# A first off-diagonal product on 32 rows that reads a transpose itself, and copies that carry half

## The chip, the cores and the metric

The kernel runs on one core of one Trainium2 chip. The metric is device microseconds of one execution: lower is better. Before the change the median of three runs is 678.3 us (677.63 to 680.24).

The engines are TensorE (PE in the profile; its weight loads are PEld), VectorE (DVE), ScalarE (ACT), GpSimd (POOL) and SyncE (SP, which issues the DMAs). Each works through its own instructions in order and waits on semaphores for the others.

## The reference

A recurrence over 768 steps for 4 batches of 8 heads of width 40, and behind it a dense layer with a quick GELU:

```python
for t in range(S):                       # S = 768, state is (B, H, 40, 40)
    y[:, :, t] = einsum('bhd,bhde->bhe', rt, state)
    Sa = einsum('bhde,bhe->bhd', state, at)
    state = state * wt[:, :, None, :] - einsum('bhd,bhe->bhde', Sa, bt)
    state = state + einsum('bhd,bhe->bhde', vt, kt)

x = y.transpose(0, 2, 1, 3).reshape(B * S, H * D)   # 3072 x 320
h = x @ w_in                                        # 320 x 2048
out = (h * (1 / (1 + exp(-1.702 * h)))) @ w_out     # 2048 x 320
```

All of it is in float32.

## The kernel before, in words

The steps are cut into 12 chunks of 64, and the batches into 2 pairs; a chunk of a pair is a *unit*, 24 in all. Within a unit the recurrence becomes matrix products: for each of the 16 pairs of batch and head there is a strictly triangular matrix N, 64x64, from the decayed a and b, and the unit needs T, the inverse of the identity plus or minus N. The state goes from one unit to the next of the same pair of batches. After two units (one chunk of all batches) the dense layer of that chunk runs: ps_up, a GELU on ScalarE (L988), ps_down.

*Cut of TensorE.* A tile of a matmul lies on 64 rows (partitions) and 64 columns of the array: a half of the partitions in, a half of the partitions out. Four such matmuls, one for each quarter, run beside each other; the code's HALF and QUARTERS name them. A float32 matmul has two records in the profile.

*The inverse (function inverse, L662 to L833).* The 64x64 matrix is cut into 32x32 blocks. The two diagonal blocks are inverted by five levels (LEVELS = 5, n = 0 to 4) of an iteration:

- Units 4 to 23 (`level`, L736): a product ps_level of EX(n) and W(n) has 64 columns for each of the 8 slots, of which the first 32 serve to make the next factor and the last 32 are T as far as it has come. L751 copies all 64 columns into W(n + 1), L753 makes E(n + 1) from the first 32 straight out of PSUM, `turned` transposes E into ES in 32x32 blocks (L702, VectorE) and spreads ES into EX (L707 on ScalarE, L709 on POOL or VectorE): column block 0 holds ES on the partitions of the upper block and zeros elsewhere, column block 1 the same for the lower block. The mask is `quads`. The last level, n = 4, multiplies the last 32 columns of W alone.
- Units 0 to 3 (`plain_level`, L758): PT holds 96 columns for each slot, a 64-wide square and 32 columns of T. L784 copies all 96 from PSUM, L723 transposes the square out of PSUM into EX. The last level multiplies the last 32 columns of PT alone.

After the last level `turned` is called once more (L790): ES(5) is the transpose of T's two diagonal blocks, and the spread of it goes into the tile T, a block-diagonal 64x64 matrix for each slot. L797 copies the blocks untransposed into Tc.

*The off-diagonal block* is then two small products. `off_one` (L801, ps_Q) multiplies P21, the lower left block of N with the whole 64 rows, by column block 1 of T, that is by ES(5) on the lower 32 rows and zeros on the upper ones. L816 or L818 mask the result into QT, `off_two` (L822, ps_T) multiplies by Tc, and L830 adds the result into T. `solved` (L899, ps_X) then uses T.

*What sets the order.* The tasks are made by `plan.add` with what they read, write and need room for. A list written out in the file (ORDER, 2700 entries) gives their order, the engine of each and the PSUM bank of each; nothing is planned anew when the kernel is built, so the change leaves order, engines and banks as they are. Waits between engines follow from the tiles that the instructions touch. PT, P21, W, E, ES, EX and T have two buffers each, one for even and one for odd units.

Of the kernel before, what the change touches and what calls it, by code (L numbers as in the profile page):

```python
# [248 lines left out]
def rwkv7_gelu_quick(ctx: ExitStack, tc: tile.TileContext, time_d, v_d, w_d, wc_d, ak_d, b_d, rv_d, w_in, w_out, out):  # L249
# [11 lines left out]
    LEVELS = 5  # L261
# [5 lines left out]
    ROUNDS, WINDOW, SHARE = 4, 5000.0, 1.0  # L267
    RANKS = [14, 16, 20, 24, 35, 37, 39, 41]
    HALF = [slice(0, 64), slice(64, 128)]
    CHANNELS = [slice(h.start, h.start + D) for h in HALF]  # L270
    BITS = (0, 1)
    QUARTERS = [(0, 0), (1, 1), (0, 1), (1, 0)]
# [7 lines left out]
    plan = Plan(dict(logw=3, wc=3, G=1, wch=3, wz=2, time=2, ak=2, b=2, rv=2, FT=3, GT=1, kh=2, bh=2, zr=2, rz=2,  # L280
                     A=1, B=1, RV=2, E0=2, W0=2, P21=2, PT=2, W=2, E=2, ES=2, EX=2, T=2, Tc=1, QT=1, zraw=2, zT=1, M=2, x=1, xT=3, g=4, ob=1), 4)
# [12 lines left out]
    def psum(t, name):  # L294
        if t.pair not in psums:
            psums[t.pair] = banks.tile([128, 2, 512], FP32, tag=f"pair{t.bank}", name=name)
        return psums[t.pair]

    def mm(o, lhsT, rhs, start):
        nc.tensor.matmul(o, lhsT, rhs, start=start, stop=True, skip_group_check=True)  # L300
# [5 lines left out]
    def pe(*sets):  # L306

        return {"PE": sum(n * 2 * max(m[0] / 1.2 + 5 if m else 58.0, cols / 1.2 + 3) for n, cols, *m in sets), "instr": sum(16 * n for n, *_ in sets)}
# [5 lines left out]
    def dve(n):  # L314
        return {"DVE": 170.0 + 1.03 * n}

    def act(n):
        return {"ACT": 210.0 + 0.76 * n}

    def any2(n):  # L320
        return {**act(n), **dve(n)}

    def copy(e):
        return nc.scalar.copy if e == "ACT" else nc.vector.tensor_copy
# [33 lines left out]
    nc.gpsimd.memset(edges, 1.0)  # L358
    for p in HALF:
        q = slice(p.start, p.start + MID)  # L360
# [17 lines left out]
    for t, one in (upper, 1.0), (later, -1.0):  # L378
        nc.gpsimd.memset(t, one)
        for p in HALF:  # L380
            select(t[p, :64], ALU.is_gt, 0, 1, 0.0)
# [24 lines left out]
    P21_t, Tc_t = several("P21", [128, 8 * 32]), several("Tc", [128, 5 * 32])  # L406
# [4 lines left out]
    EX_t, T_t, QT_t = several("EX", [128, 8, 2, 32]), several("T", [128, 8, 2, 32]), several("QT", [128, 8, 32])  # L411
# [83 lines left out]
    def load(i):  # L495
        for name, of, src, n in (("ak", ak_of, ak_d, 1024), ("b", b_of, b_d, 512), ("rv", rv_of, rv_d, 1024),
                                 ("RV", RV_of, v_d, 320), ("time", time_of, time_d, 2 * DM)):
            rows = [slice(p.start, p.start + D) for p in HALF] if name in ("ak", "b", "rv") else [slice(0, 128)]

# [38 lines left out]
    def decay(i):  # L538
# [3 lines left out]
        def by_time(t):  # L542
            ps, lw = psum(t, "ps_cum"), logw_of(i)
            for n in (1, 0):
                for b in BITS:
                    u = b ^ n
                    mm(ps[HALF[u], b, :160], incl[HALF[b]], lw[HALF[b], n * 160:(n + 1) * 160], True)
        plan.add(R, pe((1, 160)), by_time, reads=T("log"), uses=T("logw"), room=T("G"), writes=T("cum"), pair=("cum", i))

        def by_channel(t):  # L550

            ps = psum(t, "ps_cumc")
            for u, f in product(BITS, BITS):
                for b, e in QUARTERS:
                    o, h = (2 * u + f) * 65, head(e, f, b, u) * D
                    mm(ps[HALF[e], b, o:o + 65], logw_t[i % 3][HALF[b], h:h + 64], edges[HALF[b]], o == 0)

# [46 lines left out]
    at = lambda tiles, n: tiles[n % len(tiles)]  # L604
# [8 lines left out]
    def prep(i):  # L613
# [16 lines left out]
        def score_A(t):  # L630

            ps = psum(t, "ps_A")
            for b, f in product(BITS, BITS):
                for e, u in QUARTERS:
                    o, j = (2 * b + f) * 64, slot(b, u, f)
                    mm(ps[HALF[u], e, o:o + 64], khT()[CHANNELS[e], j], ahT()[CHANNELS[e], j], o == 0)
        plan.add(R + 1, pe((4, 64)), score_A, reads=T("khT", "ahT"), uses=T("ak"), room=T("A"), pair=("A", i))
# [4 lines left out]
        def score_RV(t):  # L642

            ps, rv = psum(t, "ps_RV"), rv_of(i)
            for e, b in product(BITS, BITS):
                for f, u in QUARTERS:
                    o, j = (2 * e + b) * 128, 4 * u + 2 * e + b
                    mm(ps[HALF[u], f, o:o + 64], rv[CHANNELS[f], 1, j], rv[CHANNELS[f], 0, j], o == 0)
        plan.add(R + 1, pe((4, 64)), score_RV, reads=T("rv"), room=T("RV"), pair=("RV", i))
# [12 lines left out]
    def inverse(i):  # L662
        R = 10 * i - 5
        T = lambda *names: [(n, i) for n in names]
        ahT = lambda: ak_of(i)[:, 0]
        blocks = lambda ps, n: ps[:, :, :4 * n].rearrange("p r (j t) -> p r j t", t=n)
        tiles_of = lambda t: t.rearrange("p (r j) t -> p r j t", r=2)
        every = lambda t, shape: t.unsqueeze(1).unsqueeze(1).to_broadcast(shape)
        W, E, ES, EX = (lambda n, t=t, k=k: at(t, turn(i, n, k)) for t, k in ((W_t, 5), (E_t, 5), (ES_t, 6), (EX_t, 5)))
        key = lambda name, n, k: (name, turn(i, n, k))  # L670
        within_of = lambda n: within[:, n].bitcast(UINT32)

        PT = at(PT_t, i).rearrange("p (j t) -> p j t", t=96)
# [62 lines left out]
        def level(n):  # L736
            first, last = n == 0, n == LEVELS - 1
            wide, rank = 32 if last else 64, R + 0.5 + 0.5 * n

            def go(t):  # L740
                ps, x, w = psum(t, "ps_level"), EX(n), at(W0_t, i) if first else W(n)
                for k in range(4):
                    for r, q in QUARTERS:
                        mm(ps[HALF[q], r, k * wide:(k + 1) * wide], x[HALF[r], index(n, r, q, k)].rearrange("p n t -> p (n t)"),
                           w[HALF[r], index(n, r, q, k), 64 - wide:], k == 0)
            pair = ("L", turn(i, n, 5))
            plan.add(rank, pe((4, wide)), go, reads=[key("EX", n, 5)] + (T("W0") if first else [key("W", n, 5)]),
                     room=T("T", "Tc") if last else [key("E", n + 1, 5)], pair=pair)
            if last:
                return pair  # L750
            plan.add(rank, any2(512), lambda t: copy(t.engine)(tiles_of(W(n + 1)), blocks(psum(t, ""), 64)),  # L751
                     writes=[key("W", n + 1, 5)], pair=pair)
            plan.add(rank, dve(256), lambda t: nc.vector.tensor_sub(  # L753
                tiles_of(E(n + 1)), every(two32, [128, 2, 4, 32]), blocks(psum(t, ""), 64)[:, :, :, :32]),
                     writes=[key("E", n + 1, 5)], pair=pair)
            turned(rank, lambda t: E(n + 1), dict(reads=[key("E", n + 1, 5)]), n + 1, EX(n + 1), [key("EX", n + 1, 5)])

        def plain_level(n):  # L758
            last = n == LEVELS - 1
            wide, rank = 32 if last else 96, R + 0.5 + 0.5 * n  # L760

            def go(t):
                ps, x = psum(t, "ps_level"), square(n)
                for k in range(4):
                    for r, q in QUARTERS:
                        mm(ps[HALF[q], r, k * wide:(k + 1) * wide], x[HALF[r], index(n, r, q, k)],
                           PT[HALF[r], index(n, r, q, k), 96 - wide:], k == 0)
                for r, q in QUARTERS:
                    first, hi, lo = index(n, r, q, 0), index(n, r, q, 2) - index(n, r, q, 0), index(n, r, q, 1) - index(n, r, q, 0)
                    of_k = PT[HALF[r], :, 64:].rearrange("p (a b c) t -> p a b c t", a=2, b=2)  # L770
                    bits = {4: 0, 2: 1, 1: 2}
                    fixed = 7 - hi - lo
                    picks = [slice(None)] * 5
                    picks[1 + bits[fixed]] = int(bool(first & fixed))
                    got = of_k[tuple(picks)]
                    if hi < lo:
                        got = got.rearrange("p a b t -> p b a t")
                    mm(ps[HALF[q], r, :4 * wide].rearrange("p (a b t) -> p a b t", a=2, b=2)[:, :, :, wide - 32:], ident[HALF[r]], got, False)
            pair = ("L", turn(i, n, 5))
            plan.add(rank, pe((4, wide), (1, 128)), go, reads=[key("EX", n, 5), ("PV", turn(i, n, 5))], uses=T("PT"),  # L780
                     room=T("T", "Tc") if last else [], pair=pair)
            if last:
                return pair
            plan.add(rank, any2(768), lambda t: copy(t.engine)(tiles_of(PT), blocks(psum(t, ""), 96)),  # L784
                     writes=[("PV", turn(i, n + 1, 5))], pair=pair)
            turned_square(lambda t: blocks(psum(t, ""), 96)[:, :, :, :64], dict(pair=pair), n + 1)

        for n in range(LEVELS):
            pair = plain_level(n) if i < PLAIN else level(n)
# [11 lines left out]
        def off_one(t):  # L801

            ps = psum(t, "ps_Q")
            for e in BITS:
                for b, u in QUARTERS:
                    j = 4 * u + 2 * e
                    mm(ps[HALF[u], b, e * 64:e * 64 + 64].rearrange("p (f t) -> p f t", f=2), at(P21_t, i)[HALF[b], 128 * e + 64 * u:128 * e + 64 * u + 64],
                       at(T_t, i)[HALF[b], j:j + 2, 1], e == 0)
        plan.add(R + 3.5, pe((2, 64)), off_one, reads=T("P21", "T0"), room=T("QT"), pair=("Q", i))

        def upper_rows(t):
            src = psum(t, "")[:, :, :128].rearrange("p b (e f t) -> p b e f t", e=2, f=2)
# [9 lines left out]
        def off_two(t):  # L822

            ps, QT = psum(t, "ps_T21"), at(QT_t, i).rearrange("p (b e f) t -> p b e (f t)", b=2, e=2)
            for e in BITS:
                for u, b in QUARTERS:
# [6 lines left out]
                 reads=T("T0"), writes=T("T"), pair=("T21", i))  # L833
# [296 lines left out]
```

## Time and profile before

| | |
|---|---|
| median of 3 runs | 678.3 us |
| the profiled execution | 678.87 us, span 677.2 us |
| TensorE busy | 650.6 us, 96% |
| TensorE's weight loads | 561.3 us, 83% |
| VectorE, ScalarE, POOL busy | 447.1, 330.6, 175.0 us |
| mean granted TensorE clock | 0.989 |
| ps_up and ps_down on the chain that ended last | 31% each |

A row of a group reads: line, engine, operation, tiles written and read, shapes, count, then busy microseconds and mean nanoseconds of one, then the idle time of that engine before them and what ended it. A row of the timeline begins with its start and its length in microseconds. A row of a stretch gives the busy time of each engine in it, the granted clock of TensorE as a share of full speed, the DMA engines' share and GB/s. Matmuls are recorded on L300, the helper `mm`, so they are told apart by their tiles. Their ends are modelled.

### The profile page before, as it was taken

How to read it: one execution, taken by the hardware profiler on the slowest of the kernel's cores; microseconds unless marked ns; L12 is line 12 of the kernel's file. 1: busy time of each engine (PE TensorE's matmuls, PEld its weight loads, DVE VectorE, ACT ScalarE, POOL GpSimd, SP SyncE). 2: the span in 40 equal slices, each digit the busy share in tenths (PEclk: the TensorE clock that was granted, in tenths of full speed). 3: DMA queues.
4: the chain of work that ended last, by engine and by line, in shares of the span. 5: the costliest groups of instructions: out<-in, count | busy, mean ns of one | idle time of the engine just before them, and what ended most of it. 6: DMA issues, size and time to landing. Idle time of an engine off the chain costs nothing.

```text
span 677.2 us, 42176 instructions
## 1 busy us (share of the span) xinstructions
PE 650.6 (96%) x19488; PEld 561.3 (83%) x19488; DVE 447.1 (66%) x906; ACT 330.6 (49%) x688; POOL 175.0 (26%) x204
## 2 busy tenths in 40 slices
PE   5668999999999999999999999999999999999997
PEld 5567887987987888898998898787988799899895
DVE  5686887777768668667776687868556766675001
ACT  4675955634664655554545435454454354252110
POOL 6442444224123023124123211321412321300000
PEclk9887999999999999999999999999999999999999
DMA  7883736315324224332304413513412412100100
GB/s 234 295 252 126 235 111 183 103 45 157 111 64 132 84 62 129 106 107 77 113 24 133 139 34 108 155 33 107 145 34 72 126 46 63 53 14 29 45 12 20
DMA packets 35311, 69.72 MB, mean 103 GB/s; under 512 B 5440, under 2 KB 14656, under 8 KB 35136
## 3 DMA queue, kind: packets, MB, share of 16 engines
q1 hardware_dynamic: 35136, 67.03, 32.6%
q8 instruction: 153, 2.51, 1.5%
q14 instruction: 22, 0.18, 0.1%
HBM read 59.15 MB, written 7.86 MB: 99 GB/s over the span
## 4 chain that ended last, share of the span: by engine, by line
PE 94%; ACT 2%; DVE 2%; issue 1%; DMA 1%; DVEq 0%; ACTq 0%; SPq 0%
PE ps_up L300 31%; PE ps_down L300 31%; PE ps_level L300 9%; PE ps_y L300 5%; PE ps_B L300 5%; PE ps_X L300 2%; PE ps_A L300 2%; PE ps_rz L300 2%; PE ps_N L300 2%; PE ps_RV L300 2%; PE ps_zT L300 1%; ACT PT L784 1%; PE ps_cum L300 1%; PE ps_Q L300 1%; PE ps_T L300 1%
## 5 line engine op out<-in xcount | busy, mean ns | idle before, releaser
L300 PE MATMUL ps_up<-xT_all,w_sb 64*64 64x256 f32 x3840 | 250.1, 377 | 0.4 <-PE ps_rz L300 0.2
L300 PE MATMUL ps_down<-w_sb,g 64*64 64x320 f32 x3072 | 239.5, 430 | 0.3 <-ACT zr L869 0.2
L300 PEld LDWEIGHTS ps_up<-xT_all,w_sb 64*64 64x64 f32 x3840 | 169.6, 133 | 15.3 <-issue 0.8
L300 PEld LDWEIGHTS ps_down<-w_sb,g 64*64 64x64 f32 x3072 | 133.3, 133 | 39.8 <-issue 1.3
L988 ACT ACTIVATE g<-ps_up 128x1024 f32<-128x1024 f32 x48 | 49.2, 1024 | 45.0 <-PE ps_up L300 44.6
L709 POOL TENSOR_TENSOR EX<-ES,quads 128x512 f32<-128x512 f32 x29 | 38.3, 1323 | 113.3 <-DVE ES L702 75.8
L751 ACT COPY W<-ps_level 128x512 f32<-128x512 f32 x56 | 32.7, 585 | 69.7 <-PE ps_level L300 68.0
L300 PEld LDWEIGHTS ps_level<-W,EX 64*64 64x64 f32 x2560 | 58.7, 134 | 5.8 <-DVE T L830 0.2
L300 PE MATMUL ps_level<-W,EX 64*64 64x64 f32 (+1 forms) x2560 | 55.9, 217 | 0.0
L753 DVE TENSOR_TENSOR E<-two,ps_level 128x256 f32<-128x256 f32 x80 | 33.2, 416 | 34.0 <-ACT W L751 30.3
L707 ACT ACTIVATE EX<-ES,quads 128x256 f32<-128x256 f32 x80 | 36.3, 501 | 30.5 <-DVE ES L702 29.9
L619 POOL TENSOR_TENSOR ak<-ak,FT 128x512 f32<-128x512 f32 x16 | 21.4, 1335 | 75.9 <-DMA ak<-in_ak 52.0
L300 PEld LDWEIGHTS ps_level<-PT,EX 64*64 64x64 f32 x1280 | 32.1, 146 | 8.8 <-DVE EX L723 5.7
L300 PE MATMUL ps_level<-PT,EX 64*64 64x64 f32 (+2 forms) x1280 | 34.2, 245 | 5.3 <-DVE EX L723 4.5
L702 DVE STREAM_TRANSPOSE ES<-E 128x256 f32<-128x256 f32 x80 | 35.3, 443 | 4.4
L300 PE MATMUL ps_y<-M,bh 64*64 64x104 f32 (+1 forms) x768 | 35.0, 247 | 2.4 <-issue 2.1
L300 PE MATMUL ps_y<-RV,kh 64*64 64x104 f32 (+1 forms) x768 | 34.8, 247 | 0.0
L891 ACT COPY B<-ps_B 128x416 f32<-128x416 f32 (+1 forms) x34 | 16.5, 491 | 33.8 <-PE ps_B L300 33.6
L300 PEld LDWEIGHTS ps_y<-RV,kh 64*64 64x64 f32 x768 | 28.5, 133 | 2.3 <-DVE M L907 0.5
L300 PEld LDWEIGHTS ps_y<-M,bh 64*64 64x64 f32 x768 | 27.2, 133 | 2.8 <-issue 2.3
L907 DVE TENSOR_TENSOR M<-ps_X,later 128x832 f32<-128x832 f32 (+1 forms) x24 | 23.8, 993 | 8.2 <-PE ps_X L300 8.0
L627 POOL TENSOR_TENSOR kh<-time,G 128x320 f32<-128x320 f32 x18 | 16.1, 892 | 48.5 <-PE ps_y L300 34.6
(131 smaller groups left out, 1092.9 us busy)
## 6 DMA issues: line engine op xcount, KB each, us to landing
ak<-in_ak SPq DMA_DIRECT2D x48, 160.0 KB
rv<-in_rv SPq DMA_DIRECT2D x48, 160.0 KB
time<-in_time SPq DMA_DIRECT2D x24, 320.0 KB
xT_all<-x_dram SPq DMA_DIRECT2D x48, 160.0 KB
wc<-in_wc SPq DMA_DIRECT2D x20, 264.0 KB
logw<-in_w SPq DMA_DIRECT2D x24, 160.0 KB
RV<-in_v SPq DMA_DIRECT2D x24, 160.0 KB
b<-in_b SPq DMA_DIRECT2D x48, 80.0 KB
```

The source lines that it names most:

```text
L300: nc.tensor.matmul(o, lhsT, rhs, start=start, stop=True, skip_group_check=True)
L619: plan.add(R, {"DVE": 690.0, "POOL": 1270.0, "sbuf": True}, lambda t: of(t.engine).tensor_mul(ahT(), ahT(), FT_of(i)), reads=T("ak", "FT") ...
L627: plan.add(R + 4, {"POOL": 870.0, "DVE": 490.0, "sbuf": True}, lambda t, n=n, dst=dst: of(t.engine).tensor_mul(dst(i)[:, :, :D], by_head(t ...
L702: plan.add(rank, dve(256), lambda t: nc.vector.transpose(ES(n), source(t)), writes=[key("ES", n, 6)], **reads)
L707: nc.scalar.activation(dst[:, :, h], ES(n), ACT.Copy, scale=quads[:, h, :1])
L709: of(t.engine).tensor_mul(dst, ES(n).unsqueeze(2).to_broadcast([128, 8, 2, 32]), quads.unsqueeze(1).to_broadcast([128, 8, 2, 32]))
L751: plan.add(rank, any2(512), lambda t: copy(t.engine)(tiles_of(W(n + 1)), blocks(psum(t, ""), 64)), writes=[key("W", n + 1, 5)], pair=pair)
L753: plan.add(rank, dve(256), lambda t: nc.vector.tensor_sub(tiles_of(E(n + 1)), every(two32, [128, 2, 4, 32]), blocks(psum(t, ""), 64)[:, :, ...
L784: plan.add(rank, any2(768), lambda t: copy(t.engine)(tiles_of(PT), blocks(psum(t, ""), 96)), writes=[("PV", turn(i, n + 1, 5))], pair=pair)
L891: plan.add(R, any2(4 * wide), lambda t: copy(t.engine)(dst(), some(psum(t, "")[:, :, :208])), writes=[("Bv", i)] if x and c > 0 else T("B" ...
L907: plan.add(R + 1, dve(8 * wide), lambda t: nc.vector.tensor_tensor(M_of(i)[:, :, :wide].rearrange("p (j b) n -> p b j n", b=2), some(psum( ...
L988: plan.add(-45, {"ACT": 1030.0, "table": "gelu"}, lambda t: nc.scalar.activation(g_of(c * NQ + q).rearrange("p m r n -> p r m n"), psum(t, ...
```

## The change

It has three parts.

1. *Copies behind the fourth level (n = 3).* In units 4 to 23 the copy into W(4) takes the last 32 of the 64 columns, 256 elements a partition and not 512. In units 0 to 3 the copy into PT takes the last 32 of the 96, 256 and not 768. The columns left out have no reader: the last level reads the last 32 alone, and the next factor is made straight from PSUM. 15 of the W copies and 3 of the PT copies are on ScalarE, 5 and 1 on VectorE.
2. *The first off-diagonal product multiplies 32 rows.* Both operands of ps_Q are cut to the lower 32 partitions of each half (LOWER: 32 to 63 and 96 to 127). Its matmuls have 32 rows and 64 columns; with that their place in the array is given as a tile of 32x64 and not 64x64. It still has 8 matmuls a unit of 64 columns.
3. *It reads ES(5) itself* and not the spread of it in T. So the product waits for the transpose (L702), and no longer for the spread (L707 or L709); the next transpose into that ES buffer has to wait for the product.

```diff
+    LOWER = [slice(h.start + 32, h.stop) for h in HALF]
...
-            plan.add(rank, any2(512), lambda t: copy(t.engine)(tiles_of(W(n + 1)), blocks(psum(t, ""), 64)),
+            past = 32 if n == LEVELS - 2 else 0
+            plan.add(rank, any2(512 - 8 * past), lambda t: copy(t.engine)(tiles_of(W(n + 1))[:, :, :, past:], blocks(psum(t, ""), 64)[:, :, :, past:]),
                      writes=[key("W", n + 1, 5)], pair=pair)
...
-            plan.add(rank, any2(768), lambda t: copy(t.engine)(tiles_of(PT), blocks(psum(t, ""), 96)),
+            past = 64 if n == LEVELS - 2 else 0
+            plan.add(rank, any2(768 - 8 * past), lambda t: copy(t.engine)(tiles_of(PT)[:, :, :, past:], blocks(psum(t, ""), 96)[:, :, :, past:]),
                      writes=[("PV", turn(i, n + 1, 5))], pair=pair)
...
             for e in BITS:
                 for b, u in QUARTERS:
                     j = 4 * u + 2 * e
-                    mm(ps[HALF[u], b, e * 64:e * 64 + 64].rearrange("p (f t) -> p f t", f=2), at(P21_t, i)[HALF[b], 128 * e + 64 * u:128 * e + 64 * u + 64],
-                       at(T_t, i)[HALF[b], j:j + 2, 1], e == 0)
-        plan.add(R + 3.5, pe((2, 64)), off_one, reads=T("P21", "T0"), room=T("QT"), pair=("Q", i))
+                    mm(ps[HALF[u], b, e * 64:e * 64 + 64].rearrange("p (f t) -> p f t", f=2), at(P21_t, i)[LOWER[b], 128 * e + 64 * u:128 * e + 64 * u + 64],
+                       ES(LEVELS)[LOWER[b], j:j + 2], e == 0)
+        plan.add(R + 3.5, pe((2, 64)), off_one, reads=T("P21") + [key("ES", LEVELS, 6)], room=T("QT"), pair=("Q", i))
```

## The prediction

> **What bounds the kernel now.** I read four views first: the page, busy time by stretch, the chain that ended last, and the groups of instructions.
>
> ```profile
> span 677.2 us, 42176 instructions
> PE 650.6 (96%) x19488; PEld 561.3 (83%) x19488; DVE 447.1 (66%) x906; ACT 330.6 (49%) x688; POOL 175.0 (26%) x204
> PE   5668999999999999999999999999999999999997
> ```
>
> The second line of digits is TensorE's busy share in fortieths of the span: it is short of nine tenths only in the first four slices, about 68 us, and at the very end. Busy time by stretch says the same in microseconds:
>
> ```profile
> core 0: us, PE busy (x) PEld busy (x) DVE busy (x) ACT busy (x) POOL busy (x), PEclk, DMA share, GB/s
> 0.00:70.00 70.00, 49.15 (x1720) 44.83 (x1724) 46.38 (x76) 41.45 (x107) 32.33 (x61) 0.90 0.71 222
> 70.00:600.00 530.00, 529.17 (x16192) 453.91 (x16186) 380.21 (x777) 273.39 (x558) 142.65 (x144) 1.00 0.33 99
> ```
>
> So there are two kernels in one. From 70 us on TensorE is idle for 0.83 us in 530: whatever VectorE or ScalarE saves there buys nothing, and whatever is added to TensorE's stream is added to the end. Before 70 us TensorE is idle for 20.85 us, units 0 to 3 go through their inverses with little other work beside them, and a shorter chain can count. The chain that ended last agrees:
>
> ```profile
> PE 94%; ACT 2%; DVE 2%; issue 1%; DMA 1%; DVEq 0%; ACTq 0%; SPq 0%
> ```
>
> The profiled execution took 678.87 us against a span of 677.2; the median of the three runs, 678.3, lies 0.6 us below it. The sum is made against 678.9 and then lowered by 0.6.
>
> **The change, part by part.** The groups that it touches, with the one size that stands for the shorter copies (L692 also copies 128x256 out of PSUM):
>
> ```profile
> L751 ACT COPY W<-ps_level 128x512 f32<-128x512 f32 x56 | 32.7, 585 | 69.7 <-PE ps_level L300 68.0 <-DVE E L753 1.5
> L751 DVE COPY W<-ps_level 128x512 f32<-128x512 f32 x24 | 16.3, 684 | 5.9 <-PE ps_level L300 5.2
> L784 ACT COPY PT<-ps_level 128x768 f32<-128x768 f32 x15 | 12.0, 800 | 7.2 <-PE ps_level L300 5.1 <-ACT wch L569 1.0 <-DVE EX L723 0.9
> L692 ACT COPY P<-ps_N 128x256 f32<-128x256 f32 x22 | 8.2, 371 | 23.1 <-PE ps_N L300 21.6 <-DVE PT L716 1.0 <-DVE PT L689 0.3
> L692 DVE COPY P<-ps_N 128x256 f32<-128x256 f32 x2 | 0.8, 412 | 0.0
> L300 PEld LDWEIGHTS ps_Q<-T,P 64*64 64x64 f32 x384 | 11.7, 135 | 3.8 <-ACT T L707 2.2 <-issue 0.2
> L300 PE MATMUL ps_Q<-T,P 64*64 64x64 f32 x384 | 11.3, 220 | 2.0 <-ACT T L707 2.0
> ```
>
> *Shorter copies, units 4 to 23.* One W copy in four shrinks from 512 to 256 elements: 15 on ScalarE by 585 - 371 = 214 ns, 5 on VectorE by 684 - 412 = 272 ns. That is 3.2 and 1.4 us of engine time, all behind a TensorE that does not wait. Worth 0; if the cover were gone, at most those 4.6 us.
>
> *Shorter copies, units 0 to 3.* Four PT copies go from 768 to 256 elements, on ScalarE 800 - 371 = 429 ns each. Unit 0's is on the path:
>
> ```profile
> 30.62 0.80 ACT L784 COPY PT<-ps_level 128x768 f32<-128x768 f32 x1 [0.70 <-PE ps_level L300]
> 31.45 0.72 DVE L723 STREAM_TRANSPOSE EX<-ps_level 128x512 f32<-128x512 f32 x1 [0.89 <-ACT PT L784]
> 32.22 0.67 PE L300 MATMUL ps_level<-PT,EX 64*64 64x32 f32 x32 [0.79 <-DVE EX L723]
> ```
>
> ScalarE, then VectorE, then TensorE, each idle until the one before: 0.43 us comes off here. Unit 1's copy is the same form, but VectorE has another instruction in front of the transpose:
>
> ```profile
> 37.32 0.80 ACT L784 COPY PT<-ps_level 128x768 f32<-128x768 f32 x1
> 37.58 0.48 DVE L830 SCALAR_TENSOR_TENSOR T<-ps_T,quads,T 128x256 f32<-128x256 f32 x1
> 38.15 0.72 DVE L723 STREAM_TRANSPOSE EX<-ps_level 128x512 f32<-128x512 f32 x1
> ```
>
> L830 ends at 38.06, so the transpose gains 0.09, not 0.43. The copies of units 2 and 3 come after 60 us, where TensorE is full. Copies: 0.5 us.
>
> *The wait of the first off-diagonal product.* In all 24 units TensorE stood still for it once, at unit 0 (the tile's own view, then the timeline):
>
> ```profile
>   ACT T L707: 2.0, 1
> ```
>
> ```profile
> 33.65 0.45 DVE L702 STREAM_TRANSPOSE ES<-ps_level 128x256 f32<-128x256 f32 x1
> 34.13 0.91 ACT L707 ACTIVATE T<-ES,quads 128x256 f32<-128x256 f32 x2 [0.52 <-DVE ES L702]
> 34.95 0.39 ACT L404 COPY PT<-one 128x256 f32<-128x256 f32 x1
> 35.09 0.46 PE L300 MATMUL ps_Q<-T,P 64*64 64x64 f32 x16 [1.96 <-ACT T L707]
> 35.24 0.79 ACT L784 COPY PT<-ps_level 128x768 f32<-128x768 f32 x1
> 35.39 0.81 PE L300 MATMUL ps_N<-b,ak 40*64 40x64 f32 x32
> 35.93 0.37 ACT L816 ACTIVATE QT<-ps_Q,quads 128x128 f32<-128x128 f32 x1
> 36.09 0.31 PE L300 MATMUL ps_level<-PT,EX 64*64 64x96 f32 x3
> ```
>
> The product can start when the transpose ends, at 34.10 instead of 35.09. But ScalarE still has the spread, a preset and a PT copy to do in its order, and that copy, which ends at 36.03, is what the product of 36.09 reads; QT stands behind it too. So the 0.99 us is handed back one step later: worth 0, at most 0.99. Early gain together: 0.5 us, bounds 0 and 0.43 + 0.43 + 0.99 = 1.85. The consumer of the spread that is left, L830, now waits for it directly; it was transitively behind it already. The next write into the same ES tile must now wait for the product; it follows unit i + 2's ps_N, which stands behind this product on TensorE through the P21 tile already. No DMA and no POOL work moves.
>
> *32 rows instead of 64.* The product keeps 8 matmuls of 64 columns per unit, so its stream is no shorter: rows do not set the length (a load of 40 rows for ps_rz takes 139 ns, one of 64 rows here 135). But all 9744 matmuls of the kernel before (19488 records, two for each) run on the array cut into 64x64 tiles; the changed program has 192 on 32x64 tiles, in 24 groups of 8, so the cut changes 48 times. No row of before shows a change of cut. This is what a crossing looks like without one, first TensorE, then its weight loads:
>
> ```profile
> 202.84 0.81 PE L300 MATMUL ps_up<-xT_all,w_sb 64*64 64x256 f32 x9
> 203.44 0.44 PE L300 MATMUL ps_Q<-T,P 64*64 64x64 f32 x16
> 203.67 0.64 PE L300 MATMUL ps_up<-xT_all,w_sb 64*64 64x256 f32 x8
> ```
>
> ```profile
> 203.23 0.51 PEld L300 LDWEIGHTS ps_Q<-T,P 64*64 64x64 f32 x16
> 203.62 0.46 PEld L300 LDWEIGHTS ps_up<-xT_all,w_sb 64*64 64x64 f32 x12
> ```
>
> Two overlaps are at stake. The weights of Q are loaded from 203.23 while ps_up's matmuls (to 203.65) still run; and Q's matmuls start at 203.44, 0.21 us before ps_up's end, as the next ps_up does before Q's end (203.67 against 203.88). Low end: 0, nothing is lost. High end: both overlaps of matmuls go, 2 x 0.21 a unit, 24 x 0.42 = 10.1 us. Between them: a change of cut exposes one weight load, 135 ns, and no more: 48 x 0.135 = 6.5 us. I take the middle one, because a load into another cut has to come before its matmul, while the records' ends are modelled, so that the 0.21 us may overstate what is really in flight.
>
> The Trainium skill (TensorEngine Tiling (Array Packing), Tiling Modes, Key Properties) says that changing the tiling mode, and not just the tile, drains the TensorE. It gives no time; taken literally it is the high end, and no run here shows it yet.
>
> Sum: 678.9 - 0.5 + 6.5 = 684.9, less 0.6 for the median: **684.3 us**, slower by 0.9%.
>
> **The rivals.** (a) *Full drain*: a crossing lets every matmul in flight end first, 10.1 - 0.5 = +9.6, 687.9; with the load exposed behind it as well (48 x 0.135) it would reach 694.4. For it: the overlap in the rows above is real work in flight. Against it: the modelled ends. By the Trainium skill's TensorEngine Tiling (Array Packing), Key Properties, it would be this one.
>
> (b) *The crossing is free*: then only the 0.5 us remains, 677.8, no change that can be measured (0.5% is 3.4 us, about what tells runs of this kernel apart). For it: the column cut stays 64, and the 32 rows lie within the 64 of the old tile. This is also the case in which the change does not do what it says: ScalarE and VectorE are relieved where nobody waits for them.
>
> (c) *Faster*: a granted clock that stays up. TensorE runs at half clock after idle stretches:
>
> ```profile
> 57.80:64.70 6.90, 6.40 (x172) 6.36 (x176) 4.16 (x7) 3.65 (x7) 2.00 (x2) 0.51 0.65 203
> ```
>
> If the shorter early chains kept this stretch at full clock, 3.4 us would come off; with 0.5 and a free crossing that is 674.4, faster by 0.6%. It decides only if a crossing costs under 3.9 / 48 = 81 ns. Against it: of the 20.85 us that TensorE idles before 70 us, 0.5 is a small part, and the stretch lies behind units 0 and 1, where that 0.5 arises.
>
> **How the numbers follow.** Forecast (part of the overlap lost, +2.9 to +8) 0.36; full drain 0.27; free crossing 0.25, a part of it with a small price and still within 0.5%; clock 0.06; more than a drain 0.06. Over 0.5% slower: nearly all of the forecast and the drain and the last, less what falls under 3.4 us, 0.64; within 0.5%: 0.28; faster: 0.08. The range 677.0 to 690.0 runs from the free crossing with the upper bound of the early gain nearly reached, to the full drain with a third of the load exposed; the forecast's own is 681 to 686.5.
>
> **What would show it.** Right: from 70 us on, the matmuls of ps_Q start 0.1 to 0.2 us nearer to the end of those before them than the 0.21 us of overlap above, their weight loads no longer begin under ps_up's pass, and the same on leaving; the span from 70 us to the end longer by 24 x 0.27; W copies at 371 and 412 ns behind the fourth level; ps_Q at unit 0 without ScalarE as its releaser, but the ps_level after it only 0.4 us earlier. Wrong: ps_Q groups still 0.23 us from their first matmul to the next group's; a stretch at half clock gained or lost in the first 70 us, which would move the end by more than the copies do; or TensorE idle time that appears behind 70 us on a wait that the change added.

## The result

| | median | runs |
|---|---|---|
| before | 678.95 us | 677.63 to 680.24 |
| after | 685.77 us | 684.97 to 687.17 |

The ratio is 1.0109, with an interval of 1.0086 to 1.0133: 7.4 us slower (5.8 to 9.0); the two medians themselves lie 6.8 us apart. The forecast was 684.3 against a median of then 678.3, 6.0 slower. The profiled execution took 686.01 us; its page:

```profile
span 684.4 us, 42170 instructions
PE 658.5 (96%) x19488; PEld 523.6 (77%) x19488; DVE 444.7 (65%) x906; ACT 326.7 (48%) x688; POOL 174.5 (26%) x204
PE   5787999999999999999999999999999999999997
```

TensorE is busy for 7.9 us more with the same 19488 records, while its weight loads are busy for 37.7 us less: not because there are fewer, or because one is shorter (133 ns at ps_up and ps_down, before and after), but because they lie over one another more, most of all at ps_up (155.7 us busy and not 169.6) and ps_down (112.1 and not 133.3). Why they do so far from ps_Q was not traced. VectorE and ScalarE lost 2.4 and 3.9 us of work, which shows nowhere in the time. By stretch (TensorE, weight loads, VectorE, ScalarE, POOL, clock):

```profile
0.00:70.00 70.00, 49.62 (x1654) 45.01 (x1658) 43.79 (x74) 39.33 (x102) 30.88 (x61) 0.83 0.69 219
70.00:600.00 530.00, 529.49 (x16027) 423.80 (x16024) 376.54 (x770) 268.23 (x555) 142.40 (x143) 1.00 0.33 99
```

Behind 70 us TensorE is as full as before, but gets through 16027 records in the same 530 us and not 16192. What it does there instead shows in the first product of unit 7, first TensorE, then its weight loads:

```profile
206.58 0.82 PE L301 MATMUL ps_up<-xT_all,w_sb 64*64 64x256 f32 x11
207.33 0.46 PE L301 MATMUL ps_Q<-ES,P 32*64 32x64 f32 x16
207.72 0.66 PE L301 MATMUL ps_up<-xT_all,w_sb 64*64 64x256 f32 x8
```

```profile
206.80 0.15 PEld L301 LDWEIGHTS ps_up<-xT_all,w_sb 64*64 64x64 f32 x3
207.33 0.32 PEld L301 LDWEIGHTS ps_Q<-ES,P 32*64 32x64 f32 x16 [0.39 <-issue]
207.72 0.42 PEld L301 LDWEIGHTS ps_up<-xT_all,w_sb 64*64 64x64 f32 x12
```

The loads of ps_Q no longer run under ps_up's pass: they begin at 207.33, together with their matmuls, and ps_up's modelled end is 207.40. On leaving it is the same: 207.72 against an end at 207.79. From ps_Q's start to the next ps_up it was 0.23 us and is 0.39; the overlap with the ps_up ahead was 0.21 us and is 0.07. The wait has no releaser that the profile knows; it appears among the waits of the weight loads as "issue", where before it stood at 0.2 us, once:

```profile
PEld ps_Q L301 <- issue: 5.3, 13, 0.5
```

The start times of the same matmuls in both traces give the price free of everything else: ahead of a ps_Q and behind it, the shift against before grows by 0.328 us (median of units 2 to 23, 0.29 to 0.38, from means over some 30 records on either side; with medians it is 0.32). That is 0.164 us for each change of the array's cut. Between these steps the shift stands still, but for single stalls that one trace has and the other lacks.

The copies and the wait did what they were to do:

```profile
L753 ACT COPY W<-ps_level 128x256 f32<-128x256 f32 x15 | 5.6, 371 | 13.3 <-PE ps_level L301 9.9 <-DVE ES L703 2.3 <-DVE E L755 1.1
L753 DVE COPY W<-ps_level 128x256 f32<-128x256 f32 x5 | 2.1, 418 | 1.1 <-PE ps_level L301 1.0
L301 PE MATMUL ps_Q<-ES,P 32*64 32x64 f32 x384 | 11.3, 233 | 1.0 <-DVE ES L703 1.0
```

371 and 418 ns (371 and 412 were expected), and unit 0's product waits for the transpose on VectorE and no longer for ScalarE.

### The profile page after: what moved, and what is told of

Same layout as the page of the kernel before. It is cut to its first block, busy times and chain, and to the rows that moved or that the text cites. A ratio compares the mean times of both kernels' runs of the same rounds, so it can differ in the third digit from the quotient of the medians.

```text
span 684.4 us, 42170 instructions
## 1 busy us (share of the span) xinstructions
PE 658.5 (96%) x19488; PEld 523.6 (77%) x19488; DVE 444.7 (65%) x906; ACT 326.7 (48%) x688; POOL 174.5 (26%) x204
## 4 chain that ended last, share of the span: by engine, by line
PE 93%; ACT 2%; DVE 2%; issue 1%; DMA 1%; DVEq 0%; ACTq 0%; SPq 0%
PE ps_up L301 31%; PE ps_down L301 30%; PE ps_level L301 10%; PE ps_B L301 5%; PE ps_y L301 5%; PE ps_X L301 2%; PE ps_N L301 2%; PE ps_rz L301 2%; PE ps_RV L301 2%; PE ps_A L301 1%; PE ps_Q L301 1%; PE ps_zT L301 1%; PE ps_cum L301 1%; ACT PT L787 1%; PE ps_T L301 1%
## 5 line engine op out<-in xcount | busy, mean ns | idle before, releaser
L301 PE MATMUL ps_up<-xT_all,w_sb 64*64 64x256 f32 x3840 | 246.6, 378 | 0.2 <-PE ps_rz L301 0.2
L301 PE MATMUL ps_down<-w_sb,g 64*64 64x320 f32 x3072 | 234.2, 430 | 0.3 <-ACT zr L872 0.2
L301 PEld LDWEIGHTS ps_up<-xT_all,w_sb 64*64 64x64 f32 x3840 | 155.7, 133 | 25.7 <-DVE B L897 0.5
L301 PEld LDWEIGHTS ps_down<-w_sb,g 64*64 64x64 f32 x3072 | 112.1, 133 | 56.5 <-issue 0.4
L753 ACT COPY W<-ps_level 128x512 f32<-128x512 f32 (+1 forms) x56 | 29.6, 528 | 69.6 <-PE ps_level L301 65.7
L301 PEld LDWEIGHTS ps_level<-W,EX 64*64 64x64 f32 x2560 | 55.4, 134 | 8.1 <-DVE T L833 0.2
L301 PE MATMUL ps_level<-W,EX 64*64 64x64 f32 (+1 forms) x2560 | 53.5, 217 | 0.0
L894 ACT COPY B<-ps_B 128x416 f32<-128x416 f32 (+1 forms) x34 | 16.5, 494 | 33.7 <-PE ps_B L301 33.4
L690 DVE COPY_PREDICATED PT<-within,ps_N 128x256 f32<-128x256 uint32 x40 | 17.8, 444 | 17.1 <-ACT P L693 11.4
L301 PEld LDWEIGHTS ps_y<-RV,kh 64*64 64x64 f32 x768 | 25.3, 137 | 3.5 <-DVE M L910 0.5
```

The source lines that it names most:

```text
L690: plan.add(R, dve(256), lambda t, n=n: nc.vector.copy_predicated(tiles_of(at(E0_t, i)), every(within_of(n), [128, 2, 4, 32]), blocks(psum( ...
L753: plan.add(rank, any2(512 - 8 * past), lambda t: copy(t.engine)(tiles_of(W(n + 1))[:, :, :, past:], blocks(psum(t, ""), 64)[:, :, :, past: ...
L894: plan.add(R, any2(4 * wide), lambda t: copy(t.engine)(dst(), some(psum(t, "")[:, :, :208])), writes=[("Bv", i)] if x and c > 0 else T("B" ...
```

## The experiments

The theory (A): the whole loss is the 48 changes of cut, some 0.165 us each. The rivals: it comes from the early stretch (B), from reading ES and its waits (C), from matmuls on 32 rows being slow in themselves (D), or only a change in the rows costs (F). E and G, on how the price adds up, come with the runs that test them. Each run is set against runs of the kernel before that were taken beside it:

| run | changes of cut | against before, us | step at ps_Q, us a unit |
|---|---|---|---|
| copies alone | 0 | +0.7 (-0.7 to 2.0) | 0.00 |
| ES read on 64 rows, short copies | 0 | +0.9 (-0.3 to 2.2) | 0.00 |
| the change | 48 | +7.4 (5.8 to 9.0) | 0.33 |
| 32 rows alone | 48 | +7.3 (6.0 to 8.6) | 0.32 |
| half of the matmuls on 32 rows | 48 | +8.8 (7.5 to 10.2) | 0.33 |
| 32 stationary columns | 48 | +11.2 (9.0 to 13.3) | 0.32 |
| both products on 32 rows | 96 | +14.6 (13.4 to 16.0) | 0.33, and 0.32 at ps_T |
| half on 32 rows, two and two | 96 | +16.9 (15.0 to 18.9) | 0.80 |
| half on 32 rows, in turns | 192 | +40.0 (38.1 to 42.0) | 1.77 |

The third column is the ratio's distance from one times the median of before. The step is taken as above, as a median over units 2 to 23. Of the code cuts below, the first is against the changed kernel and the others against the kernel before; they leave out what a product reads by name, and the lengths of the copies.

### The parts, one at a time

*Copies alone*: the product is that of before.

```diff
-                    mm(..., at(P21_t, i)[LOWER[b], ...], ES(LEVELS)[LOWER[b], j:j + 2], e == 0)
+                    mm(..., at(P21_t, i)[HALF[b], ...], at(T_t, i)[HALF[b], j:j + 2, 1], e == 0)
```

> The shorter copies alone; the off-diagonal product is that of the kernel before (64 rows, T). Theory A (the whole loss is the 48 changes of the array's cut, the copies are worth their early half microsecond): 0.3 to 0.6 us below the kernel before, within 0.2%, unit 0's transpose behind the copy 0.4 us earlier, and every ps_Q group 0.23 us from its first matmul to the next group's. Theory B (part of the loss comes from the early stretch, in which the changed kernel came 1.2 us later to the dense layers, because the earlier copies shift the granted clock): 0.5 to 1.5 us above the kernel before, with more than the 13.7 us at half clock that its trace shows.

Measured: no difference; A's gain of 0.3 to 0.6 us is not seen. On its spot the gain is there to the digit. The timeline of unit 0, answering to the three rows at 30.62, 31.45 and 32.22 of before:

```profile
29.82 0.37 ACT L787 COPY PT<-ps_level 128x256 f32<-128x256 f32 x1 [0.69 <-PE ps_level L301]
30.23 0.72 DVE L724 STREAM_TRANSPOSE EX<-ps_level 128x512 f32<-128x512 f32 x1 [0.46 <-ACT PT L787]
31.00 0.67 PE L301 MATMUL ps_level<-PT,EX 64*64 64x32 f32 x32 [0.37 <-DVE EX L724]
```

The copy takes 0.37 and not 0.80 us, VectorE idles 0.46 and not 0.89, TensorE 0.37 and not 0.79. Yet the first matmul of the dense layers starts at 69.5 us, where it started at 69.6. Its row gives the first and the last start; before, this run, the changed kernel:

```profile
L300 PE MATMUL ps_up<-xT_all,w_sb x3840: 372/376/427, 69.6 to 657.9; 64*64 64x256 f32 x192
```

```profile
L301 PE MATMUL ps_up<-xT_all,w_sb x3840: 372/376/427, 69.5 to 658.4; 64*64 64x256 f32 x192
```

```profile
L301 PE MATMUL ps_up<-xT_all,w_sb x3840: 373/376/427, 71.1 to 665.1; 64*64 64x256 f32 x192
```

So nothing of the 0.42 us is left at 70 us; where it goes was not traced. The time alone does not refute B, whose 0.5 to 1.5 us lie inside the interval, but at its upper end of 2.0 us it could not make the loss of 7.4. Nor does the trace look like B: the granted clock of the first 70 us is 0.95, above the 0.90 of before, and the dense layers start no later.

*32 rows alone*: long copies, and the moving operand from T.

```diff
-                    mm(..., at(P21_t, i)[HALF[b], ...], at(T_t, i)[HALF[b], j:j + 2, 1], e == 0)
+                    mm(..., at(P21_t, i)[LOWER[b], ...], at(T_t, i)[LOWER[b], j:j + 2, 1], e == 0)
```

> The 32 rows alone: both operands cut to the lower 32 rows, the moving one still read from T behind its spread, long copies. Theory A (price per change of cut): +6.5 to +8.5 us, each unit 0.33 us later behind its ps_Q than ahead of it, as in the changed kernel. Theory C (the loss comes from reading ES and its waits, not from the rows): within 1 us of the kernel before.

Measured: +7.3 us, the whole loss, with the same step of 0.32, and without the short copies or ES. C falls, and B as the cause of the loss.

*ES read on 64 rows, short copies*: the mask moves from the spread into the copy of P21, and the array keeps its cut.

```diff
-        plan.add(R, any2(256), lambda t: copy(t.engine)(<P21>, <ps_N>), ...)
+        def lower_rows(t):
+            for e in BITS:
+                if t.engine == "ACT":
+                    nc.scalar.activation(dst[:, e], src[:, e], ACT.Copy, scale=quads[:, 1, :1])
+                else:
+                    nc.vector.tensor_scalar(dst[:, e], src[:, e], quads[:, 1, :1], None, ALU.mult)
+        plan.add(R, any2(256), lower_rows, ...)
...
+                    mm(..., at(P21_t, i)[HALF[b], ...], ES(LEVELS)[HALF[b], j:j + 2], e == 0)
```

> Short copies, and the product reads ES itself, but on 64 rows: the copy of P21 is multiplied by the mask of the lower 32 rows, in two instructions, so that the upper rows of ES meet zeros. Same waits as the changed kernel and no change of cut. Theory A: 0 to 1 us below the kernel before, ps_Q groups 0.23 us long, unit 0's ps_Q at the end of the transpose. Theory C (reading ES costs): like the changed kernel, +5 us or more.

Measured: no difference from before (A's 0 to 1 us faster is not met: it is 0.9 us slower, with zero inside the interval), and no step. This run shows what the wait was worth, in the timeline of unit 0:

```profile
33.09 0.40 DVE L709 STREAM_TRANSPOSE ES<-ps_level 128x256 f32<-128x256 f32 x1
33.52 0.91 ACT L714 ACTIVATE T<-ES,quads 128x256 f32<-128x256 f32 x2 [1.05 <-DVE ES L709]
33.55 0.71 PE L301 MATMUL ps_Q<-ES,P 64*64 64x64 f32 x16 [1.54 <-DVE ES L709]
34.63 0.79 ACT L793 COPY PT<-ps_level 128x768 f32<-128x768 f32 x1
35.48 0.76 PE L301 MATMUL ps_level<-PT,EX 64*64 64x96 f32 x12 [0.35 <-ACT PT L793]
```

The product starts beside the spread and not behind it, 0.9 us sooner; the next ps_level still starts when ScalarE's copy ends, at 35.42.

### What a change of cut costs

*Half of the matmuls on 32 rows*: the first four on 32 rows, the last four on 64.

```diff
+                    rows = LOWER if e == 0 else HALF
+                    mm(..., at(P21_t, i)[rows[b], ...], at(T_t, i)[rows[b], j:j + 2, 1], e == 0)
```

> Of the 8 matmuls of each product the first 4 on 32 rows, the last 4 on 64, all from T, long copies: still 48 changes of cut, but half of the matmuls on 32 rows. Theory A (price per change of cut, 0.165 us each): as with all 8 on 32 rows, +6.5 to +8.5 us. Theory D (matmuls on 32 rows are slower in themselves): half of it, +3 to +4 us.

Measured: +8.8 us (a little above A's 6.5 to 8.5), and a step of 0.33 as with all eight. D, which wanted 3 to 4 us, falls: half as many matmuls on 32 rows, the same price.

*Two and two* has `rows = LOWER if b == u else HALF`, *in turns* `rows = LOWER if b == 0 else HALF`.

> Half of the matmuls of each product on 32 rows, in the order 32 32 64 64 32 32 64 64, all from T, long copies: 96 changes of cut and not 48. Theory A (each change costs 0.165 us): +14.5 to +17 us. Theory D (matmuls on 32 rows are slower in themselves, and the number of changes does not matter): as the run with the first half on 32 rows, +9 us.

> The same half on 32 rows, in turns 32 64 32 64 and so on: 192 changes of cut. Theory A: +28 to +33 us, a straight line through the runs with 48 and 96. Theory E (a change costs because the stream in flight has to end, and with one matmul in flight there is less to wait for): below the line, +18 to +27 us. Theory D: +9 us.

Measured: +16.9 and +40.0 us. The first is what A wanted; the second lies well above its line, not below, so E falls, and A as a plain line too. The groups of ps_Q, with half in one piece, two and two, and in turns:

```profile
L301 PE MATMUL ps_Q<-T,P 64*64 64x64 f32 x192 | 8.3, 242 | 0.0
L301 PE MATMUL ps_Q<-T,P 32*64 32x64 f32 x192 | 8.2, 241 | 2.0 <-ACT T L708 2.0
```

```profile
L301 PE MATMUL ps_Q<-T,P 64*64 64x64 f32 x192 | 15.9, 243 | 0.0
L301 PE MATMUL ps_Q<-T,P 32*64 32x64 f32 x192 | 15.9, 241 | 2.5 <-ACT T L708 2.5
```

```profile
L301 PE MATMUL ps_Q<-T,P 64*64 64x64 f32 x192 | 31.9, 247 | 0.0
L301 PE MATMUL ps_Q<-T,P 32*64 32x64 f32 x192 | 31.7, 245 | 3.2 <-ACT T L708 3.2
```

By their records the same 384 are busy for 16.5, 31.8 and 63.6 us, the two forms added (ends are modelled, so they overlap in part). In one piece four matmuls, one in each quarter, run beside each other; two and two leaves half of the quarters empty, in turns three of four. Uncut, the product takes 0.23 us for its four passes of four, 58 ns a pass. Eight passes of two cost four more, 0.23 us a unit, and sixteen of one twelve more, 0.69. Take that off the steps, and (0.80 - 0.23) / 4 = 0.14 and (1.77 - 0.69) / 8 = 0.135 us are left for a change. That reading was tried with *both products on 32 rows*, which has 96 changes and always four matmuls beside each other (ps_Q as in *32 rows alone*; here the second product):

```diff
-                    mm(..., at(Tc_t, i)[HALF[u], 32 * j:32 * j + 64], QT[HALF[u], b, e], e == 0)
+                    mm(..., at(Tc_t, i)[LOWER[u], 32 * j:32 * j + 64], QT[LOWER[u], b, e], e == 0)
```

> Both off-diagonal products on the lower 32 rows, all 8 matmuls of each, from T and QT, long copies: 96 changes of cut, and all four quarters still work beside each other. The second product leaves out the upper 32 rows of its sum. Theory A (each change costs 0.165 us, whatever the product): ps_T 0.33 us a unit later than without, as ps_Q is, +13 to +16 us in all, and less than the 16.9 us of the run with the same 96 changes inside one product. Theory G (that run's price came from the changes alone, not from quarters standing idle): +16 to +18.5 us.

Measured: +14.6 us, and steps of 0.33 at ps_Q and 0.32 at ps_T, 0.65 a unit where two and two took 0.80. A second product pays the same price, and the steps bear the reading out (the two totals alone would not: their intervals touch).

*32 stationary columns*: 64 rows, each matmul split into two of 32 columns, on 64x32 tiles.

```diff
+                    for h in BITS:
+                        mm(ps[HALF[u].start + 32 * h:HALF[u].start + 32 * h + 32, b, ...],
+                           at(P21_t, i)[HALF[b], <columns + 32 * h>:... + 32], at(T_t, i)[HALF[b], j:j + 2, 1], e == 0)
```

> All 64 rows, from T, long copies, but each matmul of the product split into two of 32 stationary columns each, on tiles of 64 rows and 32 columns: 16 matmuls a unit, still 48 changes of cut, now in the columns. Theory A (any change of the cut empties the array): +7 to +11 us, with the first weight load of ps_Q only behind the last matmul before it. Theory F (only a change in the rows does): 0 to +3 us, what the 8 more matmuls cost, and weight loads of ps_Q still under ps_up's pass.

Measured: +11.2 us, just above A's 7 to 11. TensorE and its loads at unit 7:

```profile
207.26 0.81 PE L301 MATMUL ps_up<-xT_all,w_sb 64*64 64x256 f32 x9
208.00 0.46 PE L301 MATMUL ps_Q<-T,P 64*32 64x64 f32 x32
208.38 0.45 PE L301 MATMUL ps_up<-xT_all,w_sb 64*64 64x256 f32 x4
```

```profile
208.00 0.29 PEld L301 LDWEIGHTS ps_Q<-T,P 64*32 64x32 f32 x32 [0.39 <-ACT logw L527]
```

The same picture: loads only at the end of ps_up's pass (208.07), 0.38 us from ps_Q to ps_up, a step of 0.32. So a change in the columns costs what a change in the rows costs, and F falls. One thing stays open: the profiled execution took 687.6 us, which the steps explain, and the four others 691.2 to 692.4. What those did besides has no trace.

### How the price is made up

In the changed kernel the first load behind a crossing can be set against the matmuls ahead of it, whatever their length. Ahead of it are 320 columns (ps_down) and 104 columns (ps_y), each with its TensorE rows and its load:

```profile
314.37 0.99 PE L301 MATMUL ps_down<-w_sb,g 64*64 64x320 f32 x12
```

```profile
315.29 0.21 PEld L301 LDWEIGHTS ps_Q<-ES,P 32*64 32x64 f32 x8 [0.49 <-ACT g L991]
```

```profile
358.25 0.36 PE L301 MATMUL ps_y<-M,bh 64*64 64x104 f32 x8
```

```profile
358.53 0.32 PEld L301 LDWEIGHTS ps_Q<-ES,P 32*64 32x64 f32 x16
```

The modelled ends are 315.36 and 358.61; the loads begin 0.07 and 0.08 us ahead of them, as with 256 columns (0.07) and with ps_Q's own 64 on leaving (0.07). It is so at every crossing of the changed kernel: 71 to 72 ns on entering (unit 0, whose product waits for the transpose, aside) and on leaving, where before it was 262 to 551 ns on entering and 200 to 372 on leaving. With half of the matmuls on 32 rows, where ps_Q ends on 64 rows and leaving changes no cut, it stays at 235 on leaving. So the load waits for the stream ahead to run out, less a fixed 70 ns by which the modelled ends are late or the load may be early. Behind that, the first matmul takes 265 ns in its record where one with its weights already there takes 217, and the next pass starts 107 ns behind it and not 58: some 48 ns of the load's 128 to 133 are not covered. In the single records of the unit at 207 us the last matmul of ps_Q starts at 207.573 and ps_up's first load at 207.718, 145 ns later, where a pass follows a pass at 58: 87 ns for the array to run empty. 87 and 48 make 0.135, as between the small matmuls above. Where the other 0.03 us of the mean of 0.164 lie stays open. The length of the passes ahead does not show as the reason: by the start times, entering costs 0.16 us behind ps_y's 104 columns and 0.16 to 0.21 behind ps_up's 256, leaving 0.16 behind ps_Q's own 64.

## Why the prediction was right, point by point

- *What bounds the kernel.* Right. Behind 70 us a microsecond put into TensorE's stream is a microsecond at the end, nearly: 22 units there at 0.328 make 7.2 us, and between the first and the last start of ps_up lie 594.0 us and not 588.3 (the rows above), 5.7 more. The other 1.5 us are not shown to be handed back. The trace of before has four stalls of 0.4 to 0.55 us, near 291, 320, 469 and 554 us, that the changed kernel's lacks; but the run with the copies alone, which has no change of cut, lacks three of them too (291, 469, 554), so they belong to single executions.
- *Shorter copies, worth 0 in units 4 to 23, 0.5 us early.* The first is right. Of the second the 0.42 us on the spot is right, but nothing of it arrives: the step that failed is that a gain at 32 us reaches 70 us. In the kernels here the first ps_up starts between 68.9 and 71.4 us, whatever was changed; half a microsecond drowns in that.
- *The wait of the product, worth 0.* Right, by the run that reads ES on 64 rows: the 0.9 us is handed back at the next ps_level, behind ScalarE's copy.
- *32 rows, 48 crossings of 0.135 us, 6.5 in all.* Right in place, sign and nearly in size: 0.164, so 24 x 0.328 = 7.9 us, against 7.4 (5.8 to 9.0) in the runs. Wrong in its account. It said that a crossing exposes one weight load and no more. Of the load only some 48 ns show; the larger part is that it does not begin until the stream ahead has run out. The two came to nearly the same number by chance.
- *Rival (a), full drain.* Right in kind: at every crossing looked at, the load waits for the matmuls ahead (71 to 72 ns before their modelled end). The Trainium skill (TensorEngine Tiling (Array Packing), Tiling Modes, Key Properties) says that changing the tiling mode drains the TensorE. These traces agree. Too dear in size: 0.21 us of overlap went by modelled ends, of which 0.07 stays, so 10.1 us should have been 24 x 2 x 0.14 = 6.7. With the 48 ns of load behind each it comes to 9.0, more than the 7.9 of the start times, so this sum, which rests on modelled ends, does not close.
- *Rival (b), the crossing is free.* Refuted by all six runs with crossings.
- *Rival (c), the clock.* It moved, and no run shows that it mattered:

```profile
0.00:70.00 70.00, 44.22 (x1741) 38.72 (x1742) 46.13 (x76) 41.59 (x106) 33.09 (x61) 1.00 0.72 220
```

This is the run with 32 stationary columns: full clock through the whole early stretch (before: 0.90, after: 0.83), and its first ps_up starts at 71.4 us, later than the 69.6 of before. The other traces have no order by the clock either (0.98: 68.9; 0.88: 69.2; 0.83: 71.1).

The expected sights came as described: ps_Q's loads no longer under ps_up, the copies at 371 and 418 ns, ps_level of unit 0 at the end of the copy. Only "0.4 us earlier" did not come: that ps_level started at 36.55 and not 36.09, in an execution whose granted clock was 0.50 from 27.5 to 44.5 us, where before had 0.99.

## What to carry to other kernels

A matmul on fewer rows is not a cheaper matmul, and in a stream with one cut of the array it is a dearer one: two changes of cut cost as much here, 0.33 us, as the whole product takes otherwise and half of it again. Zeros that fill a tile up to the cut of its neighbours cost nothing that could be measured here (0.9 us, interval -0.3 to 2.2), as the passes are as long anyway; move the mask into a copy, as one run does, rather than change the tile. Where cuts have to change, put all matmuls of the other cut in one piece and with all quarters at work.

## What the runs showed of the hardware that was not expected

- A change in the columns of the cut (64x64 to 64x32) costs what a change in its rows does: a step of 0.32 against 0.32 us.
- The wait for the stream to run out is named nowhere in the profile. It stands as "issue" before a weight load, or under whatever engine's name came last ("ACT logw", "ACT g" in the rows above), and TensorE's busy time covers it.
- In the first 70 us the granted clock went from 0.83 to 1.00 between executions with no order in when the dense layers begin (68.9 to 71.4 us); TensorE is idle there for some 20 us anyhow, waiting for others (before: 20.85 of 70).
